# Where x is transposed and when its highway runs: a lag of one block instead of four, all transposes on TensorE, weights loaded early

**Chip, cores, metric.** One core of one Trainium2 chip. The time is the device time of a run in microseconds (us); the span is the part of the profiled run from its first to its last instruction, about 1.7 us less. All runs compared here are in the fast state unless it is said.

## The reference, cut to what matters

```python
# q, k, v: 4 sequences x 8 heads x 768 positions x 64; float32
scores = q @ k.T / sqrt(64)
keep   = (position of key < 4) | (0 <= position of query - position of key < 128)
a      = softmax(where(keep, scores, -1e9))
x      = (a @ v), heads side by side: 3072 tokens x 512
H = maximum(x @ w_h, 0);  T = sigmoid(x @ w_t + b_t)
out = T * H + (1 - T) * x                       # a highway layer
```

The kernel works on 24 blocks of 128 tokens, six to a sequence. A block needs its own keys and those of the block before it, and the four "sink" keys of its sequence. x of a block comes out with tokens on the partitions; the highway products need it transposed.

## The kernel before

One loop drives all engines; iteration i holds pieces of several blocks, and every engine runs its pieces in program order. The pieces, with the tiles they write in PSUM:

```python
s_ps  = tile_pool("ps_s",  bufs=2, PSUM)   # scores, 2 banks each
av_ps = tile_pool("ps_av", bufs=1, PSUM)   # a @ v, 2 banks
m_ps  = tile_pool("ps_m",  bufs=2, PSUM)   # 1 bank each: tp, xtp, tps, hps, sk

for i in range(-2, NB + LAG + 1):          # LAG = 4
    m, o = i - LAG, i - LAG - 1
    ...
    pe_S(i+1, 0); act_S(i+1, 0); pe_S(i+1, 1)      # scores, exp of the first half
    dve_d(o); dve_mask(i, 1)
    pe_T(i+2)                                      # T: q and k transposed into tp
    if not by_dma(i-1): pe_X(i-1)                  # X: x transposed into xtp; by_dma(n): n >= 15
    dve_e(o); pe_A(i)                              # A: a @ v
    act_T(i+2)                                     # copy tp -> qk
    if not by_dma(i-1): act_X(i-1)                 # copy xtp -> xT
    act_S(i+1, 1); dve_mask(i+1, 0)                # exp of the second half
    dve_rec(i); dve_o(o); dve_x(i)                 # dve_o also starts the output DMA
    if by_dma(i): sp_X(i)                          # x transposed by a DMA
    pe_Mt(m); act_u(m); pe_Mh(m)                   # Mt into tps, tanh, Mh into hps
    if (i+1) % 6 in (2, 4): pe_sink(i+1)           # sink scores into sk
    ...
```

GpSimd issues all loads, one after the other; they turn float32 into float16 on the way. The order is q, k, v of blocks 0 to 2, then 4 KB of sink rows, then vs, which it builds itself from those rows, then blocks 3 and 4, wt (`x @ w_t`), block 5, wh (`x @ w_h`), and so on.

The softmax here doesn't subtract the row's maximum and nothing guards it: scores larger than these inputs give would overflow.

## Time and profile before

| | before |
|---|---|
| time, median of 4 runs | 139.93 us (139.4 to 141.31) |
| span of the profiled run | 137.6 us |
| busy: TensorE, VectorE, ScalarE, GpSimd | 115.0, 97.2, 94.1, 74.6 us |
| iteration 2, 5 and 22 begin (first score matmul) | 23.95, 39.35, 115.18 us |
| six iterations, x by TensorE / x by DMA | 27.8 / 24.3 us |

No single engine is busy throughout: the start belongs to the loads, the middle to TensorE, the end to VectorE. From the view of waits (engine and line, what it waited for: total us, times, longest) these two are the ones that the change touches:

```profile
POOL vs L130 <- DMA vd<-in_v_dram: 2.7, 1, 2.7
PE tps L319 <- ACT qk L201: 2.1, 4, 0.7
```

The first is GpSimd waiting for the sink rows. The second is Mt waiting for the copy of q and k. It reads nothing of that copy.

### The profile page before, as it was taken

Reading aid. Unit: us, or ns where it says so; the run is one execution under the profiler, and the core shown is the slowest. Engines: PE = TensorE matmul, PEld = TensorE weight load, DVE = VectorE, ACT = ScalarE, POOL = GpSimd, SP = SyncE. Lnnn points to the kernel's source line nnn. Section 1 sums busy time; section 2 is a strip of 40 time slices with the busy share of each in tenths; the row PEclk is TensorE's granted clock in tenths of the full one; section 3 lists DMA queues with packets and bytes.
Section 4 is the critical chain, followed back from the end, with each engine's and each line's share of the span. In section 5 each row is a group of like instructions: output and inputs, shape, how many; then the busy total and the mean of one; then the engine's idle time right before and its main releaser. Section 6 shows DMA issues by size and latency. Waiting matters only on the chain.

```text
span 137.6 us, 3217 instructions
## 1 busy us (share of the span) xinstructions
PE 115.0 (84%) x1276; PEld 74.4 (54%) x1276; DVE 97.2 (71%) x213; ACT 94.1 (68%) x120; POOL 74.6 (54%) x99
## 2 busy tenths in 40 slices
PE   6657519829899799999997999999999999799910
PEld 2235319719666367567664675675655777354300
DVE  6434602642478697788787977978899988979980
ACT  3057807947887997897879878978698987413300
POOL 6994799955969979999999991005000000000000
PEclk9999999995999999999999999999999999999995
DMA  0999099999999999999999999633233243333322
GB/s 5 112 125 105 0 108 147 154 167 172 157 151 147 188 196 192 136 183 200 161 196 198 193 177 183 103 114 114 90 108 89 63 119 114 98 108 104 126 102 79
DMA packets 84625, 18.19 MB, mean 132 GB/s; under 512 B 80513, under 2 KB 81537, under 8 KB 84610
## 3 DMA queue, kind: packets, MB, share of 16 engines
q0 software_dynamic: 76256, 10.51, 113.2%
q1 hardware_dynamic: 8354, 7.48, 16.7%
q8 instruction: 10, 0.16, 0.5%
q14 instruction: 5, 0.04, 0.1%
HBM read 21.01 MB, written 6.29 MB: 198 GB/s over the span
## 4 chain that ended last, share of the span: by engine, by line
PE 43%; ACT 17%; POOL 15%; DMA 10%; DVE 8%; issue 3%; POOLq 0%; DVEq 0%
PE hps L334 11%; PE tps L321 11%; ACT e L249 9%; ACT qk L201 7%; DMA ksd<-in_k_dram 7%; PE av L275 5%; POOL qsd L84 5%; PE sps L241 4%; PE tps L319 4%; POOL ksd L85 4%; POOL v L92 4%; DVE dd L340 3%; DVE ee L346 3%; DVE otok L352 3%; PE sk L219 2%
## 5 line engine op out<-in xcount | busy, mean ns | idle before, releaser
L249 ACT ACTIVATE e<-sps,ebias 128x1024 f16<-128x1024 f32 (+1 forms) x48 | 49.9, 1046 | 6.4 <-PE sps L241 6.3
L260 DVE TENSOR_TENSOR e<-e,mask 128x1024 f16<-128x1024 f16 (+1 forms) x48 | 30.9, 643 | 5.6 <-ACT e L249 5.2
L201 ACT COPY qk<-tp 128x1024 f16<-128x1024 f16 x24 | 24.1, 1002 | 13.7 <-PE tp L196 13.7
L275 PE MATMUL av<-v,e 128*128 128x112 f16 x352 | 25.4, 223 | 0.8 <-DVE e L260 0.8
L340 DVE SCALAR_TENSOR_TENSOR dd<-hps,xh 128x512 f16<-128x512 f32 x24 | 16.6, 690 | 12.6 <-PE hps L334 12.5
L334 PE MATMUL hps<-wh_sb,xT 128*128 128x512 f16 x96 | 24.6, 379 | 0.0
L321 PE MATMUL tps<-wt_sb,xT 128*128 128x512 f16 x96 | 24.6, 379 | 0.0
L84 POOL DMA_DIRECT2D qsd<-in_q_dram x24 | 22.3, 930 | 3.5 <-DMA wt_sb<-in_moe_w_t_dram 1.7
L275 PEld LDWEIGHTS <-e 128*128 128x128 f16 x352 | 21.9, 103 | 2.0 <-DVE e L260 1.2
L85 POOL DMA_DIRECT2D ksd<-in_k_dram x24 | 22.0, 916 | 1.8 <-PE sk L219 1.5
L92 POOL DMA_DIRECT2D v<-in_v_dram x24 | 22.2, 923 | 1.4 <-DMA qsd<-in_q_dram 1.1
L327 ACT ACTIVATE u<-tps 128x512 f16<-128x512 f32 x24 | 14.5, 602 | 10.6 <-PE tps L321 10.6
L241 PE MATMUL sps<-qk 64*128 64x128 f16 x352 | 15.8, 229 | 4.2 <-ACT qk L201 2.6
L241 PEld LDWEIGHTS <-qk 64*128 64x128 f16 x352 | 11.2, 99 | 11.5 <-issue 9.4
L346 DVE SCALAR_TENSOR_TENSOR ee<-u,dd 128x512 f16<-128x512 f16 x24 | 16.5, 686 | 0.5
L294 DVE TENSOR_TENSOR xh<-av,rec 128x512 f16<-128x512 f32 x24 | 16.4, 684 | 0.2
L321 PEld LDWEIGHTS <-xT 128*128 128x128 f16 x96 | 9.3, 97 | 13.0 <-issue 3.9
L352 DVE SCALAR_TENSOR_TENSOR otok<-xh,ee 128x512 f32<-128x512 f16 x24 | 15.6, 651 | 0.2
L334 PEld LDWEIGHTS <-xT 128*128 128x128 f16 x96 | 9.4, 97 | 11.8 <-issue 0.8
L194 PE MATMUL tp<-ident,qsd 128*128 128x128 f16 x96 | 10.4, 236 | 4.2 <-DMA qsd<-in_q_dram 4.0
L289 DVE RECIPROCAL rec<-av 128x8 f32<-128x8 f32 x24 | 4.9, 204 | 12.1 <-PE av L275 6.7
L196 PE MATMUL tp<-ident,ksd 128*128 128x128 f16 x96 | 10.2, 234 | 3.1 <-DMA ksd<-in_k_dram 3.1
(48 smaller groups left out, 94.5 us busy)
## 6 DMA issues: line engine op xcount, KB each, us to landing
out_dram<-otok SPq DMA_DIRECT2D x24, 256.0 KB, 2.5
qsd<-in_q_dram POOLq DMA_DIRECT2D x24, 128.0 KB, 6.0
ksd<-in_k_dram POOLq DMA_DIRECT2D x24, 128.0 KB, 6.4
v<-in_v_dram POOLq DMA_DIRECT2D x24, 128.0 KB, 6.5
wt_sb<-in_moe_w_t_dram POOLq DMA_DIRECT2D x1, 512.0 KB, 8.3
wh_sb<-in_moe_w_h_dram POOLq DMA_DIRECT2D x1, 512.0 KB, 10.0
xT<-xh SPq DMA_TRANSPOSE x9, 2.4
vd<-in_v_dram POOLq DMA_DIRECT2D x4, 4.0 KB, 5.8
```

Of the source, the lines that this page charges most:

```text
L84: nc.gpsimd.dma_start(out=qsd, in_=q[b, :, rows, :].transpose([1, 0, 2]))
L85: nc.gpsimd.dma_start(out=ksd, in_=k[b, :, rows, :].transpose([1, 0, 2]))
L92: nc.gpsimd.dma_start(out=vt[:, :, 0:D], in_=v[b, :, rows, :].transpose([1, 0, 2]))
L201: nc.scalar.copy(out=qk, in_=tp_of.pop(n))
L241: nc.tensor.matmul(sps[:, hh, o:o + P], lhsT=kk[rows, hp, :], rhs=qT[rows, hp, :], start=True, stop=True)
L249: nc.scalar.activation(out=e.rearrange("p a b c d -> p a (b c d)"), in_=sps[:, :, 0:2 * np_ * P], func=AF.Exp, bias=ebias, scale=SCALE)
L260: nc.vector.tensor_tensor(out=ev, in0=ev, in1=m.unsqueeze(1).to_broadcast([P, 4, np_ * P]), op=ALU.mult)
L275: nc.tensor.matmul(av[:, g, 2 * hl + hh, 0:_AVN], lhsT=e[:, hh, hl, pc, :], rhs=vt[:, 65 * h:65 * h + _AVN], start=first, stop=False, skip ...
L321: nc.tensor.matmul(tps, lhsT=xT[:, kc, :], rhs=wt_sb[:, kc, :], start=False, stop=(kc == NOC - 1))
L334: nc.tensor.matmul(hps, lhsT=xT[:, kc, :], rhs=wh_sb[:, kc, :], start=(kc == 0), stop=(kc == NOC - 1))
L340: nc.vector.scalar_tensor_tensor(out=dd, in0=h_of.pop(n), scalar=0.0, in1=xh_of[n], op0=ALU.max, op1=ALU.subtract)
L346: nc.vector.scalar_tensor_tensor(out=ee, in0=u_of.pop(n), scalar=1.0, in1=dd_of.pop(n), op0=ALU.add, op1=ALU.mult)
```

## The change

It means to shorten the end: the highway of block i-1 runs in iteration i, so three iterations fall away. For that, x must be transposed quickly, so TensorE does it for every block, X moves ahead of T, and ScalarE copies x early. The weights are then wanted in iteration 1, so they are loaded behind v of block 1. VectorE builds the first vs, so that GpSimd doesn't wait for the sink rows. Its core:

```diff
-    LAG = 4
-    WAT = 4
+    XBAR = ()                      # blocks whose x goes by DMA: none
...
         load_v(1)
-        load_qk(2)
+        load_sink_v(0)
+        load_w(moe_w_t, wt_sb)
+        load_w(moe_w_h, wh_sb)
...
+        load_qk(2)
         load_v(2)
-        load_sink_v(0)
+        load_qk(3)
...
-        for i in range(-2, NB + LAG + 1):
-            m, o = i - LAG, i - LAG - 1
+        for i in range(-2, NB + 2):
+            ms, os_ = highway(i), highway(i - 1)     # here: block i-1, block i-2
...
                 pe_S(i + 1, 1)
-            if on(o):
+            if on(i - 1) and i - 1 not in XBAR:
+                pe_X(i - 1)
+                act_X(i - 1)
+            for o in os_:
                 dve_d(o)
             if on(i):
                 dve_mask(i, 1)
+            if on(i + 1):
+                act_S(i + 1, 1)
             if on(i + 2):
                 pe_T(i + 2)
-            if on(i - 1) and not by_dma(i - 1):
-                pe_X(i - 1)
...
             if on(i + 2):
                 act_T(i + 2)
-            if on(i - 1) and not by_dma(i - 1):
-                act_X(i - 1)
             if on(i + 1):
-                act_S(i + 1, 1)
                 dve_mask(i + 1, 0)
...
+            if i == 0:
+                sink_ones()
+                sink_v(0, nc.vector)                 # was GpSimd, at i == -2
```

More of the change, by code (lines that the diff above doesn't have):

```diff
@@ L67 @@
     r_pool = ctx.enter_context(tc.tile_pool(name="p_r", bufs=3))
-    x_pool = ctx.enter_context(tc.tile_pool(name="p_x", bufs=LAG + 3))
+    x_pool = ctx.enter_context(tc.tile_pool(name="p_x", bufs=5))
     td_pool = ctx.enter_context(tc.tile_pool(name="p_td", bufs=3))
@@ L75 @@
     NV = AHEAD + 4
+    NS4 = H * NSINK
+    KW = NHP * P + 32
+    XBAR = ()
     v_ring = [const.tile([P, VW], FP16, tag=f"v{i}", name=f"v{i}") for i in range(NV)]
@@ L109 @@
     ones_row = const.tile([P, P], FP16, tag="ones_row")
-    NS4 = H * 4
-    KW = NHP * P + 32
     ks_bd = [const.tile([P, KW], FP16, tag=f"ks{i}", name=f"ks{i}") for i in range(2)]
@@ L126, in load_sink_v, with sink_v, load_w @@
     def load_sink_v(b):
-        nc.gpsimd.dma_start(out=vs_dn[b % 2], in_=v[b, :, 0:4, :])
-    def sink_v(b):
-        nc.gpsimd.tensor_tensor(
+        nc.gpsimd.dma_start(out=vs_dn[b % 2], in_=v[b, :, 0:NSINK, :])
+    def sink_v(b, eng):
+        eng.tensor_tensor(
             out=vs_bd[b % 2][0:NS4, :, 0:D], in0=vs_dn[b % 2].unsqueeze(1).to_broadcast([NS4, H, D]),
             in1=bm[0:NS4, :].unsqueeze(2).to_broadcast([NS4, H, D]), op=ALU.mult)
+    def load_w(w, sb):
+        nc.gpsimd.dma_start(out=sb, in_=w.rearrange("(kc p) of -> p kc of", p=P))
     with tc.manual_schedule(engines={ENG.Pool}):
@@ L143 @@
             base=0, pattern=[[1, P]], channel_multiplier=-1)
-        load_v(1)
         nc.gpsimd.affine_select(
@@ L147 @@
             base=-1, pattern=[[-1, P]], channel_multiplier=1)
-        load_qk(2)
+        load_v(1)
+        load_sink_v(0)
+        load_w(moe_w_t, wt_sb)
+        load_w(moe_w_h, wh_sb)
         nc.gpsimd.affine_select(
             out=bm, in_=bm, compare_op=ALU.is_ge, fill=0.0,
-            base=0, pattern=[[-4, H]], channel_multiplier=1)
+            base=0, pattern=[[-NSINK, H]], channel_multiplier=1)
         nc.gpsimd.affine_select(
             out=bm, in_=bm, compare_op=ALU.is_ge, fill=0.0,
-            base=3, pattern=[[4, H]], channel_multiplier=-1)
+            base=NSINK - 1, pattern=[[NSINK, H]], channel_multiplier=-1)
+        load_qk(2)
         load_v(2)
-        load_sink_v(0)
+        load_qk(3)
     nc.sync.dma_start(out=bt32, in_=moe_b_t.unsqueeze(0))
@@ L167, in more_constants @@
             nc.vector.memset(es_t[i], 0.0)
-    def late_constants():
         nc.vector.tensor_copy(out=mask0, in_=mask[:, 1, :])
@@ L186 @@
     qkT, tp_of, s_of, e_of, av_of, rec_of = {}, {}, {}, {}, {}, {}
-    xtp_of = {}
-    xh_of, xT_of, t_of, u_of, h_of, dd_of, ee_of, sk_of = {}, {}, {}, {}, {}, {}, {}, {}
+    xtp_of, xh_of, xT_of, t_of, u_of, h_of, dd_of, ee_of, sk_of = {}, {}, {}, {}, {}, {}, {}, {}, {}
     def pe_T(n):
@@ L209, in pool_sink @@
             dst = ks[rows, 0:NHP * 136].rearrange("p (a b) -> p a b", b=136)
-            nc.gpsimd.tensor_copy(out=dst[:, :, 4 * hh:4 * hh + NSINK],
+            nc.gpsimd.tensor_copy(out=dst[:, :, NSINK * hh:NSINK * hh + NSINK],
                                   in_=kT[rows, :, 0:NSINK])
@@ L354, in dve_o, with lag, highway, has_sink @@
         nc.sync.dma_start(out=out[n * P:(n + 1) * P, :], in_=otok)
-    def by_dma(n):
-        return n >= 15
     def on(n):
         return 0 <= n < NB
+    def lag(n):
+        return 2 if n in XBAR else 1
+    def highway(i):
+        return [m for m in range(NB) if m + lag(m) == i]
+    def has_sink(n):
+        return on(n) and n % NSC >= 2 and n % 2 == 0
     with tc.manual_schedule(engines={ENG.PE, ENG.DVE, ENG.Activation, ENG.SP, ENG.Pool}):
-        for i in range(-2, NB + LAG + 1):
-            m, o = i - LAG, i - LAG - 1
+        for i in range(-2, NB + 2):
+            ms, os_ = highway(i), highway(i - 1)
             if i == -2:
@@ L367 @@
                 more_constants()
-                late_constants()
-                sink_ones()
-            if on(i) and i % NSC >= 2 and i % 2 == 0:
+            if has_sink(i):
                 act_sink(i)
@@ L379 @@
                 dve_mask(i, 1)
+            if on(i + 1):
+                act_S(i + 1, 1)
             if on(i + 2):
                 pe_T(i + 2)
-            if on(i - 1) and not by_dma(i - 1):
-                pe_X(i - 1)
-            if on(o):
+            for o in os_:
                 dve_e(o)
@@ L396 @@
                 dve_rec(i)
-            if on(o):
+            for o in os_:
                 dve_o(o)
@@ L400 @@
                 dve_x(i)
-                if by_dma(i):
+                if i in XBAR:
                     sp_X(i)
-            if on(m):
+            for m in ms:
                 pe_Mt(m)
@@ L406 @@
                 pe_Mh(m)
-            if on(i + 1) and (i + 1) % NSC >= 2 and (i + 1) % 2 == 0:
+            if has_sink(i + 1):
                 pe_sink(i + 1)
+            if i == 0:
+                sink_ones()
+                sink_v(0, nc.vector)
             if on(i + 2) and (i + 2) % NSC == 0:
-                pool_sink((i + 2) // NSC)
-                sink_v((i + 2) // NSC)
+                b = (i + 2) // NSC
+                pool_sink(b)
+                if b:
+                    sink_v(b, nc.gpsimd)
+                if b + 1 < B:
+                    load_sink_v(b + 1)
             for n in (range(3, AHEAD + 1) if i == -2 else [i + 2 + AHEAD]):
                 if n < NB:
-                    load_qk(n)
+                    if n > 3:
+                        load_qk(n)
                     load_v(n)
-                if n == WAT:
-                    nc.gpsimd.dma_start(out=wt_sb, in_=moe_w_t.rearrange("(kc p) of -> p kc of", p=P))
-                if n == WAT + 1:
-                    nc.gpsimd.dma_start(out=wh_sb, in_=moe_w_h.rearrange("(kc p) of -> p kc of", p=P))
-            b = i // NSC + 1
-            if i >= 0 and i % NSC == 1 and b < B:
-                load_sink_v(b)
 _INS = ['q', 'k', 'v', 'n_sink', 'window', 'moe_w_h', 'moe_w_t', 'moe_b_t']
```

## The prediction

> **What bounds the kernel now.** I read the page's slices first, then the chain of waits in order of time, then the timeline of ScalarE and TensorE in one steady iteration, then sums over windows. Below, "iteration i" is one turn of the main loop. In it TensorE computes scores S(i+1) in two groups, transposes q and k of block i+2 (call it T), transposes x of block i-1 (X), multiplies by v for block i (A), and does the two highway products Mt and Mh of block m. Today m = i-4, afterwards m = i-1.
>
> The slices of the page:
>
> ```profile
> PE   6657519829899799999997999999999999799910
> DVE  6434602642478697788787977978899988979980
> ACT  3057807947887997897879878978698987413300
> DMA  0999099999999999999999999633233243333322
> ```
>
> There are three regimes. Until slice 11 (38 us) TensorE has holes while DMA is full, except slice 4, where DMA moves nothing. From there to slice 34 TensorE is full. In the last slices only DVE is.
>
> The hole in slice 4 and the tail, from the chain:
>
> ```profile
> 11.24 3.08 DMA vd<-in_v_dram
> 14.49 1.03 POOL vs L130
> ...
> 25.72 10.05 DMA ksd<-in_k_dram
> 35.82 0.40 PE tp L196 x4
> ...
> 132.20 0.70 DVE ee L346
> 132.93 0.69 DVE otok L352
> ```
>
> GpSimd stands still for the small sink load and then builds vs itself, so it issues no load from 11.8 to 15.5 us. k of block 6 lands at 35.8 us and is the last load that TensorE waits for on this chain. The last output arithmetic ends at 133.6; the span ends 4.0 us later (output DMA and end).
>
> One steady iteration from the chain (us from the start, length):
>
> ```profile
> 75.92 0.35 PE sps L241 x8
> 76.27 0.02 issue
> 76.30 1.11 ACT e L249
> 77.41 0.91 ACT qk L201
> 78.32 0.04 issue
> 78.36 0.38 PE tps L319
> 78.74 0.86 PE tps L321 x4
> 79.60 0.86 PE hps L334 x4
> ```
>
> and ScalarE in the same iteration:
>
> ```profile
> 76.30 1.11 ACT L249 ACTIVATE e<-sps,ebias 128x1024 f16<-128x1024 f32 x1 [0.54 <-PE sps L241]
> 77.31 1.00 ACT L201 COPY qk<-tp 128x1024 f16<-128x1024 f16 x1
> 78.20 0.60 ACT L313 COPY xT<-xtp 128x512 f16<-128x512 f16 x1
> 78.67 1.14 ACT L249 ACTIVATE e<-sps,ebias 128x1024 f16<-128x1024 f32 x1
> 79.68 0.62 ACT L327 ACTIVATE u<-tps 128x512 f16<-128x512 f32 x1
> ```
>
> Start to start, an exp holds ScalarE 1.01 us, the q/k copy 0.89, the x copy 0.47. Mt waits for the q/k copy because it writes into the same PSUM buffer: the pool m has two, used in turn in the order tp, xtp, tps, hps, so tps takes tp's and hps takes xtp's. The loop S, exp, q/k copy, Mt, Mh, S closes in 4.54 us (75.92 to 80.46).
>
> Sums over two windows of six iterations each, with x transposed by TensorE (first) and by DMA (second; blocks from 15 on):
>
> ```profile
> 41.83:69.66 27.83, 26.53 (x327) 17.53 (x326) 22.59 (x44) 24.04 (x34) 26.63 (x34) 1.00 2.10 179
> 92.88:117.15 24.27, 24.23 (x296) 15.71 (x294) 21.85 (x42) 20.62 (x27) 1.76 (x3) 1.00 0.34 99
> ```
>
> The columns are length, then busy time of PE, PEld, DVE, ACT, POOL. So 4.64 us per iteration with TensorE's transpose, 4.04 without; in the second TensorE never stands still (24.23 of 24.27).
>
> **What the Trainium skill says.** "PSUM — Partial Sum Buffer", Specifications: 8 banks of 2 KiB per partition. The kernel's pools use all: scores 2 buffers of 2 banks, av 2 banks, m 2 of 1 bank. So a third m buffer is not there, in either kernel. "TensorE: Matmul & The Clock Gate", section on the 16 sub-arrays, says that ScalarE and VectorE are strictly first in, first out; the trace agrees, ScalarE ran the five instructions above in program order. So program order on ScalarE decides when a PSUM buffer comes free. "Perfetto Trace Analysis", Optimization Strategy: a gap that repeats on the engine that should be full can mean too few PSUM buffers; the 0.32 us that TensorE waits before Mt at 78.36 is such a gap. The first-named page, "What's actually happening", says that the clock rises after a busy window of about 3.4 us; the trace agrees, four transposes take 0.61 us up to 22 us and 0.40 from 24.6 us.
>
> **The change part by part.**
>
> *The last iterations.* The loop is three turns shorter. Today S of iteration 22 begins at 115.25 us and 22.3 us follow; the last four outputs come 2.1 us apart, bound by three DVE operations of 0.69 each. Afterwards, from the same point: iteration 22 has no T and takes 4.0; in iteration 23 DVE runs behind TensorE: d(21), mask, e(21), rec(23), o(21), x(23) end 7.9 after the start; X(23) with its copy ends at 9.1; Mt and Mh take 0.38 + 0.86 + 0.86 and end at 11.2; d, e, o of block 23 take 2.1 and end at 13.4; plus the 4.0 at the end: 17.4. Saved: 4.9 us.
>
> *Transposes back on TensorE.* Nine blocks lose the DMA transpose: 36 transposes (0.25 us per block on TensorE) and 9 copies (0.47 effective, 4.2 us on ScalarE) come in.
>
> *The new order on ScalarE.* This is what decides. Per iteration it becomes exp, x copy, second exp, q/k copy, tanh. The pool's order becomes xtp, tp, tps, hps: Mt now needs the x copy, which is early, but Mh writes into tp's buffer and needs the q/k copy, which is now last. From the start of the first exp: 1.01 + 0.47 + 1.01 + 1.00 = 3.49 us to the end of the q/k copy, 0.04 for the signal, Mh 0.16 of refill + 0.86, the first group of S 0.35, 0.02: 4.92 us per iteration. TensorE alone would reach Mh about 0.7 us earlier. ScalarE can't use that time, since the next exp needs S, which stands behind Mh in TensorE's order. So 4.92 replaces 4.54 for blocks up to 14 and 4.06 or so after them. A turn with sink scores adds 0.53 (today 79.60 + 0.86, then 0.51 and the es activation) and gives 5.45. A turn in which S is of the first block of a sequence has exps of half the size and stays bound by TensorE at 4.13 (today 67.25 to 71.38). Six turns: 3 x 4.92 + 2 x 5.45 + 4.13 = 29.8, against 27.8 and 24.3 today.
>
> *The start.* GpSimd gets back 3.7 us of issuing. But 1 MB of weights goes ahead of q of block 2. Today k5 lands at 30.7 and wh at 34.1, with v5 between; q and k land 0.84 apart, so one weight costs about 2.5 us of transfer. With v1 landing at 10.7: 2 x 2.5 + 2 x 0.84 gives k2 at 17.4 (today 13.0), S(2) begins at 19.1 (today 1.7 after k2), k3 is there at 19.9, A(1) ends at 23.0, Mt and Mh with a clock that is still rising take 2.6, sink scores 0.5: iteration 2 begins at 26.2 us. It was 23.95 today, but today's iterations 3 and 4 then wait for DMA (k5 lands at 30.7, k6 at 35.8) and iteration 5 begins at 39.4. Afterwards no load is late: iteration 5 begins at 26.2 + 4.92 + 5.45 + 4.92 = 41.5. The highways of three more blocks are then done, which is what the tail saves; the start itself loses 2.1.
>
> *The sum.* From iteration 2 to 22: 4.92 + 5.45 + 4.92 + 4.13 = 19.4; twelve turns 59.6; 18 to 21 20.7; together 99.7. 26.2 + 99.7 + 17.4 = 143.3 us of span, 5.7 more than today. As a check: start +2.1, iterations 5 to 22 84.5 against 75.9, so +8.6, tail -4.9: +5.8. The profiled run took 139.27 with a span of 137.6, so 1.7 outside: 145.0 us.
>
> **Rivals.** *The tail and the start decide.* If the loop kept 4.54 throughout (Mh not held, say because the q/k copy is in time), 16 turns would be 0.38 shorter: 6 us less, 139 us, the same. For it: ScalarE's own work is only 4.0 us a turn and TensorE's about 4.3, so nothing but the wait forbids it. Against: the buffer order in the code leaves no way round. *A better start.* If all waits of the first 36 us vanish and the weights share DMA with q2 at little cost, iteration 2 could begin at 24 and the loop run at TensorE's 4.3: 134 us. For it: DMA moved nothing in slice 4. Against: weights must pass before block 2. *Colder and later.* If TensorE's clock stays low through iteration 1, or the gaps before Mh lower it again, 2 to 4 us more: 148. DVE as new bound I discard: 4.05 us of work a turn.
>
> **Range and chances.** The loop is the sturdiest term (durations read off, order given): a tenth of a us on 17 turns is 1.7 us. The start may be off by 2, the tail by 1. 141.3 to 148.2. Slower by over 2% begins at 142.2; most of the range lies above. I leave 0.15 for within 2% and 0.08 for faster.
>
> **What would show it.** Right: a wait of hps (L334's counterpart) on the q/k copy, about 0.6 us, in some 16 turns; full turns of 4.9 us also for late blocks; iteration 2 at about 26 us with no DMA wait after; 2 last DVE triples close together. Wrong: no such wait, or turns of 4.5 or less; then the tail's 4.9 us decide and the kernel is level or faster.

## The result

The changed kernel takes 146.05 us (median of 4 runs, 145.33 to 146.7) against 139.93: the ratio is 1.042, with a 95% interval of 1.032 to 1.052. Ratios here are the mean time of one kernel's fast runs over that of the other's of the same rounds, so they are not quite the ratio of the medians.

| | before | after | predicted after |
|---|---|---|---|
| iteration 2 begins | 23.95 | 28.06 | 26.2 |
| iteration 5 begins | 39.35 | 43.37 | 41.5 |
| iteration 22 begins | 115.18 | 128.49 | 125.9 |
| span | 137.6 | 145.0 | 143.3 |
| start to iteration 5 | 39.4 | 43.4 (+4.0) | +2.1 |
| iterations 5 to 21 | 75.8 | 85.1 (+9.3) | +8.6 |
| from iteration 22 to the end | 22.4 | 16.5 (-5.9) | -4.9 |

The table takes both columns from the profiled runs. That of the changed kernel is the slowest of its fast runs (146.7 us), that of the kernel before is a little below its lowest (139.27 us), so the spans differ by 7.4 us where the medians differ by 6.1.

The end became shorter as meant, and more than that was lost in the middle. The slices of the page after (busy share of each fortieth of the span, in tenths):

```profile
PE   6632069989889988988899789889897988998840
ACT  3176029497787877977976797798769778976310
DMA  1999999999999999999929999210221021021111
```

TensorE's row of nines has turned into eights with nines: it has gaps in every iteration. Before, slices 11 to 37 were nines but for three sevens (the prediction shows that row). DMA has no empty slice at the start any more. The chain of waits (start, length, what) of one full iteration of the changed kernel:

```profile
77.82 0.35 PE sps L243 x8
78.19 1.11 ACT e L251
79.31 0.47 ACT xT L315
79.78 1.02 ACT e L251
80.80 0.91 ACT qk L203
81.75 1.02 PE hps L336 x4
82.77 0.35 PE sps L243 x8
```

All of it runs on ScalarE except Mh and the first scores: exp, x copy, exp, q/k copy, then Mh, then the next scores. From one score matmul to the next it is 4.95 us. Mt (tps) is not on the chain any more; it runs beside ScalarE. The waits:

```profile
DVE dd L342 <- PE hps L336: 26.2, 24, 1.5
...
PE hps L336 <- ACT qk L203: 9.4, 17, 0.7
```

Seventeen times Mh waits for the q/k copy, on average 9.4 / 17 = 0.55 us. VectorE's wait for hps was 12.5 us before, and it is 14.3 us in experiment 1, where Mh isn't held; what comes on top of that here is the same delay passed on. Six iterations, one sequence after the other (length, then busy time of PE, PEld, DVE, ACT, POOL):

```profile
42.42:72.44 30.02, 26.87 (x326) 17.67 (x326) 22.56 (x42) 23.96 (x33) 21.13 (x26) 1.00 1.93 166
72.44:102.47 30.03, 26.88 (x327) 17.67 (x327) 22.57 (x42) 23.97 (x33) 12.55 (x16) 1.00 0.98 106
```

30.0 us for six, early and late alike. TensorE is busy 26.9 of them and ScalarE 24.0: nobody is full, which is what a loop through two engines looks like. In the second row DMA is half as busy (0.98 against 1.93) and the length is the same, so the loads play no part here.

### The profile page after: what moved, and what is told of

The parts are those of the page before. It is cut to its first block, busy times and chain, and to the rows that moved or that the text cites. A ratio compares the mean times of both kernels' runs of the same rounds, so it can differ in the third digit from the quotient of the medians.

```text
span 145.0 us, 3266 instructions
## 1 busy us (share of the span) xinstructions
PE 115.4 (80%) x1312; PEld 74.8 (52%) x1312; DVE 96.9 (67%) x214; ACT 98.0 (68%) x129; POOL 73.6 (51%) x98
## 4 chain that ended last, share of the span: by engine, by line
ACT 41%; PE 35%; POOL 7%; DMA 5%; issue 5%; DVE 4%; POOLq 0%; DVEq 0%
ACT e L251 25%; PE hps L336 16%; ACT qk L203 11%; DMA ksd<-in_k_dram 5%; PE tps L323 4%; ACT xT L315 4%; PE av L277 4%; PE sps L243 4%; DVE dd L342 3%; PE sk L221 3%; POOL qsd L85 2%; PE tps L321 1%; POOL ksd L86 1%; POOL v L93 1%; PE tp L198 1%
## 5 line engine op out<-in xcount | busy, mean ns | idle before, releaser
L342 DVE SCALAR_TENSOR_TENSOR dd<-hps,xh 128x512 f16<-128x512 f32 x24 | 16.6, 692 | 26.2 <-PE hps L336 26.2
L85 POOL DMA_DIRECT2D qsd<-in_q_dram x24 | 22.4, 932 | 7.6 <-PE tp L198 5.0
L277 PE MATMUL av<-v,e 128*128 128x112 f16 x352 | 24.4, 218 | 0.7 <-DVE e L262 0.7
L277 PEld LDWEIGHTS <-e 128*128 128x128 f16 x352 | 21.3, 101 | 1.1 <-DVE e L262 0.9
L243 PE MATMUL sps<-qk 64*128 64x128 f16 x352 | 14.8, 225 | 2.6 <-ACT qk L203 2.6
L348 DVE SCALAR_TENSOR_TENSOR ee<-u,dd 128x512 f16<-128x512 f16 x24 | 16.5, 686 | 0.2
L196 PE MATMUL tp<-ident,qsd 128*128 128x128 f16 x96 | 9.9, 230 | 7.2 <-DMA qsd<-in_q_dram 6.9
L243 PEld LDWEIGHTS <-qk 64*128 64x128 f16 x352 | 10.7, 98 | 9.4 <-issue 7.3
L315 ACT COPY xT<-xtp 128x512 f16<-128x512 f16 x24 | 13.7, 572 | 1.0 <-PE xtp L310 1.0
L212 POOL COPY ks<-qk 64x16 f16<-64x16 f16 x8 | 1.6, 201 | 21.1 <-ACT qk L203 20.9
```

The costliest lines, as they stand in the source:

```text
L85: nc.gpsimd.dma_start(out=qsd, in_=q[b, :, rows, :].transpose([1, 0, 2]))
L243: nc.tensor.matmul(sps[:, hh, o:o + P], lhsT=kk[rows, hp, :], rhs=qT[rows, hp, :], start=True, stop=True)
L277: nc.tensor.matmul(av[:, g, 2 * hl + hh, 0:_AVN], lhsT=e[:, hh, hl, pc, :], rhs=vt[:, 65 * h:65 * h + _AVN], start=first, stop=False, skip ...
L315: nc.scalar.copy(out=xT, in_=xtp_of.pop(n))
L342: nc.vector.scalar_tensor_tensor(out=dd, in0=h_of.pop(n), scalar=0.0, in1=xh_of[n], op0=ALU.max, op1=ALU.subtract)
```

## The experiments

Twelve kernels ran, each in 5 rounds beside the kernel before on the same chip; all gave correct results. The medians of the kernel before in the four sets are 139.58, 139.85, 139.37 and 139.47 us, so the times can be compared across sets to within some tenths.

### 1. The q/k copy before the second exp

```diff
                 dve_mask(i, 1)
-            if on(i + 1):
-                act_S(i + 1, 1)
...
                 act_T(i + 2)
             if on(i + 1):
+                act_S(i + 1, 1)
                 dve_mask(i + 1, 0)
```

> The changed kernel with one reordering on ScalarE: the q/k copy before the second exp instead of after it. All instructions, buffers, loads and matmuls stay. Theory (Mh waits for the q/k copy because it takes over its PSUM buffer): the 17 waits of hps on the q/k copy, 9.4 us, vanish; the copy ends 2.9 us after the first exp starts instead of 3.5 and later; a full turn falls from 4.95 us to about 4.35, now bound by TensorE; six turns from 30.0 to about 27; the time from 146.05 to about 136 (134.5 to 138). Rival (ScalarE simply has more to do, nine more copies and exps in the way): same work, so 145 to 146.

Measured: 137.33 us, 8.7 less than the change, ratio to before 0.987 (0.982 to 0.993). The wait of hps on the q/k copy is gone from the view of waits. Six iterations of this run by windows:

```profile
43.19:70.33 27.14, 26.42 (x331) 17.71 (x332) 22.57 (x42) 24.07 (x33) 21.69 (x28) 1.00 2.10 185
```

27.14 instead of 30.02 with the same instructions: TensorE is busy 26.42 of 27.14. ScalarE's work is unchanged (24.07), so the rival, that the added copies cost the time by being work, falls. This one order turns a loss of 4% into a gain of 1%, which by the bound of 2% counts as the same time as before.

### 2. The sink part alone, in the kernel before

```diff
-                sink_v((i + 2) // NSC)
+                if i + 2:
+                    sink_v((i + 2) // NSC, nc.gpsimd)
+            if i == 0:
+                sink_v(0, nc.vector)
```

> The kernel before with one part of the change alone: vs of the first sequence is built by VectorE in iteration 0, so GpSimd no longer waits for the first sink load; everything else, also the place of the weights, as before. Theory (until 36 us the kernel before is a chain of GpSimd's issues and loads): GpSimd gains the 2.66 us of standing and the 1.03 of vs, so k of block 6 lands some 3 us earlier, the loop reaches its steady state that much earlier, and the time falls by 2.5 to 3.7 us to about 136.5. Rival (the transfers set the start, not the issues; the hole is filled later anyway): within 1 us of 139.9.

Measured: 135.38 us, ratio 0.973 (0.968 to 0.978): 4.2 us less than before, more than the 2.5 to 3.7 expected. Iteration 5 begins at 35.78 us instead of 39.35, so 3.6 us of it are in the start, where they were expected. The rival falls. This part of the change is good by itself.

### 3. The whole start of the change, in the kernel before

```diff
         load_v(1)
+        load_sink_v(0)
+        <load wt>; <load wh>          # were behind blocks 4 and 5
...
         load_qk(2)
         load_v(2)
+        load_qk(3)
```

(with the edit of experiment 2, and GpSimd's mask instructions in the order of the change)

> The kernel before with the whole start of the change (weights ahead of q of block 2, mask order, sink part), its loop with a lag of 4 kept. Theory (1 MB of weights ahead of block 2 holds back T(2) from 12.2 to about 18.8 us and S(3) from 24 to about 26, but afterwards no load is late): iteration 5 begins at about 38 instead of 39.4, so 138 to 139; the weights' place gives back most of what the sink part gains. Rival (the start of the change is good as a whole and only the loop is bad): as the sink part alone or better, 135 to 136.5.

Measured: 139.29 us, ratio 1.002 (0.997 to 1.006); iteration 5 begins at 39.27, where about 38 was expected. Moving the weights forward costs 3.9 us against experiment 2 and cancels its gain, somewhat more than expected ("most of" it). With a lag of 4 nobody wants the weights so early.

### 4. The late blocks by DMA again, in the change

```diff
-    XBAR = ()
+    XBAR = tuple(range(15, 22))
```

> The changed kernel with x of blocks 15 to 21 transposed by DMA, two iterations behind (its own switch). Theory (the order of ScalarE decides, the transposes themselves matter little): without the x copy a full turn is 1.01 + 1.01 + 1.00 + 0.04 + 1.02 + 0.37 = 4.45 us instead of 4.95, five such turns save 2.5, the turn without a highway saves 1, the two highways in iteration 23 cost 2: 144 to 145. The wait of hps on the q/k copy stays in these turns. Rival (the nine transposes and copies brought back are the loss, so turns fall to the 4.04 us that they had before): 7 x 0.9 = 6 us less, 140.

Measured: 143.44 us, 2.6 less than the change, ratio 1.031 (1.026 to 1.036). hps still waits for the q/k copy 16 times (8.3 us). The full iterations without X take 4.47 us (104.43 to 108.90), as worked out, and not the 4.04 that the kernel before has there. So seven of the nine transposes brought back, with their copies, are 2.6 us of the loss, not 6.

### 5. The weights behind k of blocks 2 and 3, in the change

```diff
-        load_w(moe_w_t, wt_sb)
-        load_w(moe_w_h, wh_sb)
...
         load_qk(2)
+        load_w(moe_w_t, wt_sb)
         load_v(2)
         load_qk(3)
+        load_w(moe_w_h, wh_sb)
```

> The changed kernel with only the place of the weights different: wt goes behind k of block 2 and wh behind k of block 3, instead of both behind v of block 1. ScalarE's order as in the change. Theory (both weights ahead of block 2 hold T(2) back by some 5 us, and that is what iteration 2 beginning at 28 us instead of 24 comes from): q and k of block 2 land near 13, of block 3 near 18, iteration 2 begins at 24 to 25, and the time falls by 3 to 4 us to 142 to 143; the turns stay at 30.0 us for six. Rival (the start is covered by what follows, since loads and highways overlap): less than 1 us, 145 to 146.

Measured: 145.73 us, only 0.3 less than the change. The expectation was wrong. TensorE's timeline of this run (start, length, engine, what, and in brackets the idle time before it and what ended it):

```profile
13.48 0.61 PE L196 MATMUL tp<-ident,qsd 128*128 128x128 f16 x4 [0.99 <-DMA qsd<-in_q_dram]
15.55 0.61 PE L198 MATMUL tp<-ident,ksd 128*128 128x128 f16 x4 [1.47 <-DMA ksd<-in_k_dram]
...
20.67 0.61 PE L196 MATMUL tp<-ident,qsd 128*128 128x128 f16 x4 [1.83 <-DMA qsd<-in_q_dram]
```

T of block 2 does come 4 to 5 us earlier (18.77 in the change), but T of block 3 only 2.0 (22.68 there): wt now passes before q of block 3 instead of before q of block 2. The clock took back most of the rest. TensorE's Mt and Mh of block 0 took 1.91 and 1.77 us here, against 1.36 and 1.03 in the change: by the lengths of these matmuls TensorE had its full clock only from about 27.0 us on (26.1 in the change). Iteration 2 begins at 27.68 us instead of 28.06. That difference alone would prove nothing: experiment 4, whose start is that of the change, had matmuls of full speed from 24.2 us on and began iteration 2 at 26.66. The medians carry the result. That the place hardly matters because the weights are needed in iteration 1 anyway, wherever they stand before it, is an argument; the moment at which the clock comes is a rival that no run here separates.

### 6. Both corrections

The edits of 1 and 5 together.

> The changed kernel with both corrections, q/k copy before the second exp and the weights behind k2 and k3. If the two causes are separate, the gains add: 146.05 - 8.7 - 3.5 = 133.8 (132.8 to 135). If they share time (TensorE full from the start on, so that an earlier start only meets a later load), 135 to 137.

Measured: 136.4 us, ratio 0.975 (0.970 to 0.980). The gains did not add to 133.8; it is 0.9 below experiment 1, and in the 135 to 137 of the second case. After experiment 5 that is no surprise.

### 7. Both corrections, and blocks 15 to 20 by DMA

The edits of 6 and `XBAR = tuple(range(15, 21))`.

> As the run with both corrections, and x of blocks 15 to 20 transposed by DMA two iterations behind. Now that TensorE bounds the turns, taking 4 transposes and a wait out of a turn must show, unlike in the run with this switch alone: turns of about 4.05 instead of 4.35, six of them, 1.7 us; the missing highway of iteration 16 comes back as a second one in iteration 22. 132 if so; if the DMA transpose or the double highway makes a new wait, as in the other or slower.

Measured: 135.15 us, 1.25 less than experiment 6; 1.7 was expected. The 132 was missed by 3 us, mostly because it was counted from the 133.8 that experiment 6 did not reach. A full iteration without X takes 4.07 us (107.06 to 111.13), where one with X takes 4.29 in experiment 6 (108.75 to 113.04). Both are shorter than the 4.47 of experiment 4, where Mh still waited.

### 8. The kernel before with a lag of 2

```diff
-    LAG = 4
+    LAG = 2
```

with the sink part and the weights placed as in experiment 5.

> The kernel before (q/k copy first, DMA transposes from block 15 on) with its lag 2 instead of 4, the sink part of the change, and the weights behind k2 and k3. Theory (the short tail is worth its 2.1 us per iteration in any loop order that does not hold Mh): against the sink part alone (135.4) two iterations of the tail less, 4.2 us, minus what the two more early highways cost while TensorE's clock is low (up to 2): 131 to 133.5. Rival (the shorter lag itself makes the loop slower): 135 or more.

Measured: 135.88 us, ratio 0.971 (0.965 to 0.977): not better than the sink part alone (135.38). The expectation was wrong. Iteration 5 begins at 40.21 us here and at 35.78 there: 4.4 us later, about what two iterations of the end are worth (2 x 2.1). The highways that no longer stand at the end stand at the front, and the weights with them. How much is due to each is not shown: against experiment 2 both the lag and the place of the weights changed, and in experiment 3 the weights alone, put still further forward, moved iteration 5 by 3.5 us. The loop was not made slower: from iteration 5 to iteration 22 it takes 75.86 us in both runs. So the rival's reason falls, though its number came.

### 9. X ahead of T in the kernel before, with the sink part

```diff
+            if on(i - 1) and not by_dma(i - 1):
+                pe_X(i - 1)
             if on(i + 2):
                 pe_T(i + 2)
-            if on(i - 1) and not by_dma(i - 1):
-                pe_X(i - 1)
...
+            if on(i - 1) and not by_dma(i - 1):
+                act_X(i - 1)
             if on(i + 2):
                 act_T(i + 2)
-            if on(i - 1) and not by_dma(i - 1):
-                act_X(i - 1)
```

> The kernel before with the sink part, and X ahead of T on TensorE and the x copy ahead of the q/k copy on ScalarE, lag 4 and DMA transposes from block 15 as before. Theory (which product gets which buffer decides): Mt now takes the x copy's buffer, free 2 us after the turn begins, and Mh that of the q/k copy, free after 2.9, both before TensorE gets there; the wait of tps on the q/k copy goes, turns up to block 14 fall from 4.54 to 4.35, ten of them, 2 us: 133.5 (133 to 134.5). Rival (that wait was paid by TensorE's fill in any case): 135.4 as the sink part alone.

Measured: 133.97 us, ratio 0.960 (0.955 to 0.964). The wait of tps on the q/k copy is gone, and six iterations fall from 27.84 us in experiment 2 to 27.14. This order of ScalarE (exp, x copy, q/k copy, exp) is the same as in experiment 1, and so is the length of six iterations, with a lag of 4 instead of 1. Together with experiment 10 this is the fastest kernel.

### 10. As 9, each weight one block later

```diff
-    WAT = 4
+    WAT = 5
```

> As the run before it in this list, and each weight one block later in the order of loads. With lag 4 the weights are wanted only in iteration 4; today block 5 waits for wt and block 6 for wh. If the load order sets the start, one weight (2.5 us of transfer) passes behind k of block 6 and the loop is up to 2 us earlier: 131.5 to 133. If Mh of iteration 4 then waits for wh, nothing is gained: 133.5.

Measured: 134.01 us, ratio 0.958 (0.954 to 0.963), which is not to be told from experiment 9. In the profiled runs iteration 5 begins at 33.51 us instead of 36.31. But from Mh of iteration 5 to that of iteration 8 it takes 15.2 us instead of 13.45 (37.06 to 52.26 against 39.87 to 53.32, starts of Mh), and GpSimd's loads stand on the chain there. Mh of iteration 4 also waited 0.9 us for wh, the second case of the expectation. Of the 2.8 us by which iteration 5 is earlier, 1.75 were given back to later loads; the 1.06 left is what these two profiled runs differ by (133.4 and 132.3 us), and that of experiment 9 was its slowest run.

### 11. T ahead of X on TensorE, in the change

```diff
                 pe_S(i + 1, 1)
+            if on(i + 2):
+                pe_T(i + 2)
             if on(i - 1) and i - 1 not in XBAR:
                 pe_X(i - 1)
                 act_X(i - 1)
...
-            if on(i + 2):
-                pe_T(i + 2)
```

> The changed kernel with T ahead of X on TensorE, so that the buffers change owners: tp comes first, Mt takes it and waits for the late q/k copy, Mh takes xtp's. ScalarE's order, all work and all data stay. Theory (the wait comes from the buffer that is handed over, nothing of Mt or Mh reads the copy): the wait moves from hps to tps and now holds Mt and Mh both: a full turn is 3.49 + 0.04 + 1.24 + 0.86 + 0.37 = 6.0 us instead of 4.95; with some 17 such turns 161 to 167. Rival (ScalarE's order alone decides, whoever owns the buffer): 145 to 147.

Measured: 146.92 us. The theory's number was missed by 14 us, and the rival's 145 to 147 came. TensorE's timeline of one iteration:

```profile
80.53 0.38 PE L321 MATMUL tps<-bt,ones_row 128*128 128x512 f16 x1 [0.29 <-ACT xT L315]
80.75 1.02 PE L323 MATMUL tps<-wt_sb,xT 128*128 128x512 f16 x4
82.45 0.81 PE L336 MATMUL hps<-wh_sb,xT 128*128 128x512 f16 x3 [0.68 <-ACT qk L203]
```

Although tp is now filled first, hps still waits for its copy. So either the two buffers don't go round in the order in which TensorE fills them, or the wait has nothing to do with buffers. The next run tells these apart.

### 12. One buffer for tp, tps and sk, the other for xtp and hps, in the change

```diff
-    m_ps = tile_pool(name="ps_m", bufs=2, PSUM)
+    ma_ps = tile_pool(name="ps_ma", bufs=1, PSUM)    # wps, tp, sk, tps
+    mb_ps = tile_pool(name="ps_mb", bufs=1, PSUM)    # xtp, hps
```

> The changed kernel with the two PSUM buffers of pool m fixed to their users: one for tp, tps and sk, the other for xtp and hps. Order of instructions, data and loads stay as in the change. It asks again what the run with T ahead of X should have asked (there the wait stayed with hps, so the buffers had not changed owners with TensorE's order). Theory (the wait comes only from the buffer handed over, since neither Mt nor Mh reads the q/k copy): the 17 waits leave hps and appear at tps, where they hold both products: 3.49 + 0.04 + 1.24 + 0.86 + 0.37 = 6.0 us for a full turn, 1.05 more in 17 turns and about 0.75 more in 3: 163 to 168 us. Rival (the wait on the q/k copy comes with ScalarE's order whoever owns the buffer): hps waits on, 145 to 148.

Measured: 171.27 us (168.56 to 171.8); by the rule of 1.5% above the fastest, only the runs of 168.56 and 169.63 (the profiled one) count as fast, so no ratio is given. The waits of this run:

```profile
PE tps L322 <- ACT qk L204: 28.9, 21, 1.9
```

and one iteration of its chain:

```profile
91.99 0.91 ACT qk L204
92.90 0.04 issue
92.94 0.38 PE tps L322
93.32 0.86 PE tps L324 x4
94.18 0.86 PE hps L337 x4
```

hps waits no more, tps does, and Mt and Mh now both stand behind the copy: 86.91 to 92.94 is 6.03 us for one iteration, as worked out. Nothing differs from the change but who owns which buffer. So the wait is the hand-over of a PSUM buffer, and the rival falls. It came in 21 iterations where 17 were counted on, and the two fast runs are 0.6 and 1.6 us above the top of the expected range. A side effect of single buffers is in the time too: X waited for VectorE to read hps, which the change doesn't have.

```profile
PE xtp L311 <- DVE dd L343: 5.2, 15, 0.8
```

In experiment 11, then, tps had got xtp's buffer although xtp was filled second. In the change, experiment 11, the kernel before and experiment 9 alike, the buffer that is copied out first goes to the first that asks for one. That fits all four; which rule the framework follows was not looked into further.

## Why the prediction was right

The measured 146.05 us lies in the range of 141.3 to 148.2, near the 145.0 predicted; "slower by over 2%" had 0.77.

**The new order on ScalarE.** Right, and the deciding step. The loop was worked out at 4.92 us and is 4.95; six iterations at 29.8 and are 30.0; the wait was to come in some 16 iterations with about 0.6 us and came in 17 with 0.55. Experiment 1 takes it away by order alone and experiment 12 moves it by ownership alone, so it is shown from both sides. One sentence of this step was wrong: the pool's two buffers are not "used in turn" in the order in which TensorE fills them (experiment 11). The conclusion drawn from it was right, since in both kernels the x copy and the q/k copy stand in the same order as X and T.

**Half-size iterations.** Put at 4.13 us, measured 4.36 (43.37 to 47.73). The chain of the changed kernel there:

```profile
42.42 1.04 PE hps L336 x4
43.48 0.70 DVE dd L342
44.22 0.38 PE tp L196 x4
```

T waits until VectorE has read hps, because it takes hps's buffer. The term missed is that read. Three such iterations are 0.7 us.

**The transposes back on TensorE.** Right in kind: experiment 4 gives 2.6 us back for seven of the nine blocks; a full iteration falls by 0.48 us, the 0.47 of the x copy that stood ahead of the q/k copy.

**The start.** Right in direction, too small: iteration 2 was put at 26.2 us and began at 28.06. k of block 2 was to land at 17.4 us and landed at 19.6, in the chain of the changed kernel:

```profile
12.07 7.49 DMA ksd<-in_k_dram
19.60 0.62 PE tp L198 x4
```

The weights are the term that was too small. wt was issued at 8.28 and took 6.7 us to land, wh at 9.05 and 8.8 us: they landed at 15.0 and 17.85, where 13.2 and 15.7 had been worked out. k2 landed 1.7 us after wh, just as allowed. By windows of this run the DMA engines moved 69 GB/s from 10 to 11 us and about 180 from 11 to 14. At 180 GB/s a weight of 512 KB takes 2.9 us (an estimate), not 2.5; that and the slack at 10 us are part of the miss. The clock was not worse than allowed: from T(2) at 19.6 it took 8.5 us to iteration 2, where 26.2 - 17.4 = 8.8 had been allowed; so the late load is the whole of the miss in this run. Experiments 4, 11 and 12 have the same loads: their transposes of k2 began at 19.27, 20.38 and 19.91 us, all late, and iteration 2 at 26.66, 28.73 and 28.48. How much of the late load reaches iteration 2 thus varies with the moment of the full clock, and the 28.06 is one run's value.

**Weights before block 2.** The prediction blamed their place. With the kernel before's lag that is so (experiments 2 and 3, 3.9 us). With the lag of one it is not: experiment 5 moved them and got 0.3 us. It may be that what costs is that they are wanted in iteration 1 at all; no run shows that.

**The end.** Predicted -4.9, measured -5.9: iteration 22 to the end took 16.5 us where 17.4 had been worked out. Of the 0.9 us by which this was worked out too long, 0.6 is the stretch after the last arithmetic: it took 3.4 us (141.6 to 145.0), and 4.0 had been allowed. The shorter end is not a gain by itself. Experiment 8 shortens the end by two iterations and loses 4.4 us at the start. The likely reason, besides the weights moved in the same run, is that a highway that leaves the end, where VectorE needs 2.1 us for it, has to be done earlier, where TensorE needs about as much (0.22 + 0.86 + 0.86).

**The rivals.** "The tail and the start decide" would have held without the wait: experiment 1 gives 137.3, where it said 139. "A better start" at 134 was not reached by the change, but a better start is what the sink part alone was worth (experiment 2). "Colder and later" did not come: the granted clock is 1.00 in both rows of six iterations above, so the gaps before Mh did not lower it, and the slow clock of iteration 1 had been allowed for.

**What stays open.** The rule by which the framework hands out the buffers; what else made the first weight land 1.8 us later than worked out; how the loss at the start in experiment 8 divides between the highways and the weights; and whether keeping TensorE's clock high between 10 and 26 us, where several runs have it at half (0.50), would be worth something. None of the runs asks that.

## What to carry to other kernels

When two products share a few PSUM buffers with transposes, look at which copy frees the buffer that each product takes, and put the copy for the earlier product first and no long instruction ahead of the other one. An engine that is only 68% busy can still set the pace if its order makes another engine wait, and reordering it costs nothing. A shorter tail is worth only what the moved work finds free at its new place, so ask first what that place is waiting for.

## What the Trainium skill lacked or had wrong

- "Perfetto Trace Analysis", Optimization Strategy, reads a repeated gap as a possible lack of buffers. Here the gap of 0.55 us in 17 iterations was such a wait for a buffer, but it went without any buffer more, by the order of ScalarE alone (146.05 to 137.33 us). Among the causes of a repeated gap the page names the number and size of buffers, not the order in which they are released.
- "TensorE: Matmul & The Clock Gate", Part 4: PE-mode transpose, says that the full clock does not engage for transposes and gives about 275 ns for one in a kernel. In the changed kernel four transposes took 0.61 us at 18.77 us, where the granted clock was 0.50, and 0.39 us at 28.84 us, where it was 1.00 (a single one 219 ns in the median, 314 ns the longest). So among matmuls a transpose does follow the clock; whether transposes alone would raise it no run asks.
- No page that I read says that GpSimd's issue of a load waits for an earlier one in flight. In both profiles it did: q of block 4 in the change waited 1.66 us for wh, q of block 7 before waited 1.72 us for wt, each time the eighth load before it. Whether the chip or the framework's semaphores ask for this, the runs don't show.
